# A searched order for a fused attention and gated-MLP kernel: every piece of work named, freely ordered, with PSUM banks and copy engines dealt by the same search

## The chip, the cores and the metric

The kernel runs on one core of a Trainium2 chip. The metric is the device time of one execution in microseconds (us). With one core there is no second die to compare with; an execution counts as slow when it lies over 1.5% above the fastest of its kernel. Every run of a changed kernel quoted here is in the fast state. The kernel before was not always: its executions spread from 307 to 314 us, and 11 of the 37 on record are slow. That is why each comparison below uses the fast runs of the kernel before from the same chip and the same rounds.

## The reference, cut to what matters

```python
def phi(x):                                   # q and k: 8 x 8 x 576 x 64
    proj = np.einsum('bhsd,df->bhsf', x, w_phi)
    proj = proj - np.max(np.abs(proj), axis=-1, keepdims=True)
    return np.concatenate([np.exp(proj), np.exp(-proj)], axis=-1)
q_p, k_p = phi(q), phi(k)
kv  = np.einsum('bhsf,bhsd->bhfd', k_p, v);   z = np.sum(k_p, axis=2)
num = np.einsum('bhsf,bhfd->bhsd', q_p, kv)
den = np.einsum('bhsf,bhf->bhs', q_p, z)[..., None] + 1e-06
x   = (num / den), heads side by side         # 8 x 576 x 512
h = gelu_tanh(x @ w_in);  u, v = halves of h
v_n = (v - mean) / sqrt(var + 1e-06) * g_ln   # layer norm over the features
v_s = np.einsum('ts,bsd->btd', w_sg, v_n) + b_sg
out = x + (u * v_s) @ w_out
```

## The kernel before

The kernel is cut into 1659 pieces, each with a kind (one letter) and a block (one digit, the batch). A long string names the order in which the program records them. Each engine then runs its own pieces in that order; between engines semaphores keep the data dependencies that the recorded order implies.

```python
def op(kind, b, f, *args):
    pieces.setdefault(kind + str(b), []).append((f, args))
...
for x in map("".join, zip(ORDER[::2], ORDER[1::2])):
    f, args = pieces[x].pop(0)                # pieces of one kind and block: first come, first served
    f(*args)
```

Three groups of pieces carry the argument. The first is the k and q projection of one slot and four heads ("n"), whose k result, one PSUM bank of 128x512, has three readers: a maximum on DVE ("r") and two exponentials on ACT ("e", one for each sign).

```python
def project(j, i, n0, n1, h0, h1):            # piece "n"
    kk, qq = ps1(), ps1()                     # two PSUM banks, taken from the string BANKS
    ...
def reduce(j, i, name, dst, n0, n1, h0, h1):  # piece "r": DVE
    src = T[name, b, j, i]
    ...
    nc.vector.tensor_reduce(out=dst[:, n0, h0:h1], in_=src.rearrange("p (h x) -> p h x", h=4),
                            axis=AX.X, op=ALU.max, apply_absolute_value=True)
def exps(j, i, e, n0, n1, h0, h1):            # piece "e": ACT
    ...
    src = T["kk", b, j, i]
    nc.scalar.activation(out=kp[:, e, 4 * i:4 * i + 4].rearrange("p h x -> p (h x)"), in_=src, func=AF.Exp,
                         scale=(1.0, -1.0)[e])
```

The second is the gathering of `w_sg`, 15 small copies on DVE with an inner step of 5 ("Q"), and beside it POOL's products of v with the exponential factors ("s").

```python
def pick(m):                                  # piece "Q": DVE, SBUF to SBUF
    ...
    nc.vector.tensor_copy(out=wp[0:nr, n0:n1].rearrange("p t (i j) -> p t i j", j=2),
                          in_=w9[:, :, :, m:m + 6:5])
def times(e, x0, n0, n1, h0, h1):             # piece "s": POOL, SBUF to SBUF, 128x1024
    ...
    nc.gpsimd.tensor_tensor(out=VX[e][:, h0:h1, x0:x0 + nn, 0:64], in0=T["vs", b][:, h0:h1, n0:n1, :],
                            in1=VX[e][:, h0:h1, x0:x0 + nn, 64:65].broadcast_to([128, hh, nn, 64]), op=ALU.mult)
```

The third is the copies whose engine is free: `move` and `engine` take the next letter of a string (v for DVE, a for ACT, p for POOL).

```python
def engine(usual):
    return {"v": nc.vector, "a": nc.scalar, "p": nc.gpsimd}[next(alts, usual)]
```

## Time and profile before

| | kernel before |
|---|---|
| median before the prediction, 3 runs | 308.34 us (307.46 to 310.44) |
| span of the profiled run | 305.4 us |
| busy, whole span: PE, DVE, ACT, POOL | 261.5, 253.1, 249.7, 161.3 us |
| busy share from 40 to 240 us: PE, DVE, ACT | 94%, 91%, 97% |
| ACT table loads | 28 |

The page's busy lines, the stretches and the chain are read in the prediction. Three more views also belong here and are shown here for the comparison later. First the gathering copies by form (line, engine, operation, shapes, count, then busy us, mean ns of one, idle us before them):

```profile
L316 DVE COPY wp<-wn 128x384 f16<-128x384 f16 x4 | 1.5, 380 | 0.0
L316 DVE COPY wp<-wn 64x128 f16<-64x128 f16 x4 | 1.2, 303 | 0.0
L316 DVE COPY wp<-wn 128x128 f16<-128x128 f16 x4 | 1.2, 297 | 0.0
```

Then the waits between the two readers of the k bank (who waited, on whom: us in all, times, longest):

```profile
DVE MX L388 <- ACT kp L407: 2.5, 3, 1.4
...
ACT kp L407 <- DVE MX L388: 0.2, 1, 0.2
```

DVE and ACT read the same 72 banks, and in the whole run they held each other up for 2.7 us. How that looks in time (start, us, what, idle before it in brackets):

```profile
22.68 4.65 ACT L407 ACTIVATE kp<-banks 128x512 f16<-128x512 f32 x9
...
23.87 6.06 DVE L388 TENSOR_REDUCE MX<-banks 128x4 f32<-128x512 f32 x10
```

Nine exponentials in a row on ACT lie beside ten maxima in a row on DVE, with no idle time on either: neither waits for the other.

### The profile page before, as it was taken

The numbers are of one execution on the slowest core, as the hardware profiler recorded it, in microseconds if no ns is written. First come the engines' busy times: TensorE is split into PE (matmuls) and PEld (weight loads), VectorE is DVE, ScalarE is ACT, GpSimd is POOL, SyncE is SP. The second block draws the span as 40 slices with busy tenths as digits, with TensorE's granted clock in tenths as the row PEclk, the third lists the DMA queues.
The fourth block names the chain that finished last, engine by engine and source line by source line (L and its number), as shares of the span: only waits on it lengthen the run. The fifth ranks groups of instructions, "written<-read, shape, count | busy, mean of one in ns | idle before, by whom it ended". The sixth has DMA issues, their size and how long they took to land.

```text
span 305.4 us, 8083 instructions
## 1 busy us (share of the span) xinstructions
PE 261.5 (86%) x3209; PEld 157.7 (52%) x3209; DVE 253.1 (83%) x606; ACT 249.7 (82%) x428; POOL 161.3 (53%) x155
## 2 busy tenths in 40 slices
PE   0146298897789999999998999999999999999993
...
DVE  3289849997899699999899899998998796877862
ACT  0049489999899899999999999999999989994210
POOL 8763999937058924803289567042694360044100
...
GB/s 160 221 205 197 59 42 222 173 192 144 255 55 0 123 228 265 105 150 278 190 79 12 45 236 5 256 126 71 13 26 141 115 29 71 2 78 29 38 108 165
DMA packets 60550, 37.48 MB, mean 123 GB/s; under 512 B 31648, under 2 KB 57184, under 8 KB 60512
## 3 DMA queue, kind: packets, MB, share of 16 engines
...
q0 software_dynamic: 22816, 11.81, 30.5%
q8 instruction: 25, 0.41, 0.6%
...
## 4 chain that ended last, share of the span: by engine, by line
PE 44%; ACT 23%; DVE 13%; POOL 8%; DMA 7%; issue 4%; ACTq 0%; DVEq 0%; SPq 0%; POOLq 0%
PE banks L681 9%; ACT kp L407 7%; PE banks L610 5%; POOL vx L424 5%; ACT qp L516 4%; PE banks L707 4%; DVE MX L388 4%; PE banks L530 4%; PE banks L479 4%; PE banks L506 4%; PE banks L660 4%; PE banks L382 3%; DMA qks<-in_k_dram 3%; ACT uT L673 2%; ACT vt L619 2%
## 5 line engine op out<-in xcount | busy, mean ns | idle before, releaser
L424 POOL TENSOR_TENSOR vx<-vs,vx 128x1024 f16<-128x1024 f32 (+1 forms) x48 | 77.9, 1645 | 53.5 <-ACT vx L414 45.4
L388 DVE TENSOR_REDUCE MX<-banks 128x4 f32<-128x512 f32 x144 | 91.8, 677 | 5.7 <-PE banks L382 2.6
L407 ACT ACTIVATE kp<-banks 128x512 f16<-128x512 f32 x144 | 77.7, 634 | 1.7 <-PE banks L382 1.4
L516 ACT ACTIVATE qp<-banks 128x1024 f16<-128x1024 f32 (+1 forms) x90 | 72.8, 904 | 1.9 <-PE banks L530 0.9
L681 PE MATMUL banks<-WsgT,vt 128*128 128x512 f16 (+1 forms) x256 | 38.6, 286 | 0.6 <-DVE uT L696 0.2
L382 PE MATMUL banks<-wk,qkT 64*128 64x128 f16 x288 | 30.5, 232 | 7.8 <-DVE qkT L143 5.2
L382 PEld LDWEIGHTS <-qkT 64*128 64x128 f16 x576 | 18.9, 100 | 26.5 <-issue 19.3
L610 PE MATMUL banks<-Win,xT 128*128 128x512 f16 x128 | 31.4, 379 | 0.7 <-DVE xT L143 0.3
L660 PE MATMUL banks<-xT,Win 128*128 128x512 f16 x128 | 32.0, 380 | 0.0
L530 PE MATMUL banks<-kvz,qp 128*128 128x65 f16 x640 | 29.7, 194 | 2.3 <-ACT qp L516 0.9
L550 DVE TENSOR_TENSOR xs<-banks,rd 128x256 f16<-128x256 f32 x80 | 31.1, 411 | 0.6
L530 PEld LDWEIGHTS <-qp 128*128 128x128 f16 x640 | 25.3, 98 | 11.3 <-issue 2.9
L382 PE MATMUL banks<-wq,qkT 64*128 64x128 f16 x288 | 29.7, 232 | 1.0 <-DVE MX L388 1.0
L479 PE MATMUL banks<-vx,kp 128*128 128x65 f16 x640 | 28.4, 195 | 1.2 <-POOL vx L424 0.9
L479 PEld LDWEIGHTS <-kp 128*128 128x128 f16 x640 | 24.7, 99 | 6.5 <-issue 1.2
L696 DVE TENSOR_TENSOR uT<-banks,uT 128x512 f16<-128x512 f32 x32 | 21.8, 685 | 6.2 <-PE banks L681 5.8
L208 PE MATMUL banks<-ident,qk 128*128 128x128 f16 x112 | 11.8, 277 | 16.8 <-DVE qk L143 16.5
L707 PE MATMUL banks<-Wout,uT 128*128 128x512 f16 x96 | 25.9, 379 | 0.0
L506 PE MATMUL banks<-qkT,wqm 66*128 66x512 f16 x72 | 22.8, 383 | 3.6 <-DMA qkT<-hl 2.1
L651 POOL TENSOR_TENSOR vt<-vt,g_bc 128x1024 f16<-128x1024 f16 x7 | 15.6, 2222 | 19.1 <-DVE vt L645 19.1
L681 PEld LDWEIGHTS <-vt 128*128 128x128 f16 x256 | 17.0, 98 | 14.7 <-issue 1.2
L407 ACT ACT_TABLE_LOAD x6 | 7.7, 1283 | 19.6 <-DVE qkT L143 19.5
...
## 6 DMA issues: line engine op xcount, KB each, us to landing
...
```

Of the source, the lines that this page charges most:

```text
L382: nc.tensor.matmul(dst, qkT[p:p + 64, n, h, :], w[p:p + 64, :], start=True, stop=True)
L388: nc.vector.tensor_reduce(out=dst[:, n0, h0:h1], in_=src.rearrange("p (h x) -> p h x", h=4), axis=AX.X, op=ALU.max, apply_absolute_value=True)
L407: nc.scalar.activation(out=kp[:, e, 4 * i:4 * i + 4].rearrange("p h x -> p (h x)"), in_=src, func=AF.Exp, scale=(1.0, -1.0)[e])
L424: nc.gpsimd.tensor_tensor(out=VX[e][:, h0:h1, x0:x0 + nn, 0:64], in0=T["vs", b][:, h0:h1, n0:n1, :], in1=VX[e][:, h0:h1, x0:x0 + nn, 64:65 ...
L479: nc.tensor.matmul(T["pkv", b, h // 3][:, c:c + 65], kp[:, e, x, :], VX[e][:, h, sh if n == SH else n, :], start=(n == 0), stop=(n == SH))
L506: nc.tensor.matmul(d, wqm[0:66, :], T["qkT", b][0:66, n, h:h + 4].rearrange("p h x -> p (h x)"), start=True, stop=True)
L516: nc.scalar.activation(out=dst, in_=T["pp", b, n, s], func=AF.Exp, scale=(1.0, -1.0)[e])
L530: nc.tensor.matmul(dst[h // 4][:, 65 * (h % 4):65 * (h % 4) + 65], qp[:, e, h, :], kvz[:, h, e, :], start=(e == 1), stop=(e == 0))
L610: nc.tensor.matmul(pv, T["xT", b][:, c, n * 128:n * 128 + 128], Win[:, c, DF2:DFF], start=(c == 0), stop=(c == 3))
L660: nc.tensor.matmul(pu, Win[:, c, d * 128:d * 128 + 128], T["xT", b][:, c, :], start=(c == 0), stop=(c == 3))
L681: nc.tensor.matmul(dst, lhs[:, d * 128:d * 128 + 128], WsgT[:, m, t0:t1], start=(m == 0), stop=(m == 4))
L707: nc.tensor.matmul(po, u[:, d, cs], Wout[:, d, :], start=False, stop=(d == 3))
```

## The change

Its intent is to find, by a long search, an order in which no engine waits. Each piece now has its own name (kind, block, number), so pieces of one kind and block can swap; the PSUM banks and the engines of the free copies come out of the same search. No piece is added or removed. The three strings are new from end to end.

```diff
+INDEX = "0123456789abcdefghijklmnopqrstuvwxyzABCDEFGHIJKLMNOPQRSTUVWXYZ"
 ALTS = (
-    "pvvpvvavvvvaavapvvvvaavvaaavvvvavvaaavvvavavvvvaaaavvvaavvvaavvvvvvvvpvaapppavvvvpavpvaavvavvvvaavvavppvapaa"
...
 ORDER = (      # 1659 names of two characters become 1659 names of three
...
 BANKS = (      # 500 digits, all dealt anew
...
     def op(kind, b, f, *args):
-        pieces.setdefault(kind + str(b), []).append((f, args))
+        n = count[kind + str(b)] = count.get(kind + str(b), -1) + 1
+        pieces[kind + str(b) + INDEX[n]] = (f, args)
...
-            if i == e == 0:                      # three such places: whichever piece comes first takes the tile
+            if ("kp", b, j) not in T:
...
-    for x in map("".join, zip(ORDER[::2], ORDER[1::2])):
-        f, args = pieces[x].pop(0)
+    for x in map("".join, zip(ORDER[::3], ORDER[1::3], ORDER[2::3])):
+        f, args = pieces.pop(x)
         f(*args)
```

More of the change, by code (lines that the diff above doesn't have):

```diff
@@ L30 @@
 VPOOL = ()
+INDEX = "0123456789abcdefghijklmnopqrstuvwxyzABCDEFGHIJKLMNOPQRSTUVWXYZ"
 ALTS = (
-    "pvvpvvavvvvaavapvvvvaavvaaavvvvavvaaavvvavavvvvaaaavvvaavvvaavvvvvvvvpvaapppavvvvpavpvaavvavvvvaavvavppvapaa"
-    "aavvavaavvavavavapvpvvvpa"
+    "aavvavvavapavavvvvvvavvvvvppavaavvvvvvvpvpppaaavvaavvvpvppavvvavvvaavapvppppavvvavvavvpvvvavpavvvavpvpvpvvvv"
+    "vvvpaappaavvavvvvvapvvvpa"
 )
 ORDER = (
-    "F0v0a0v0a0v0a0D0a0a0a0a0a0a0a0m0a0a0L0m0a1t0F0t0a1a1a1c0m0c0n0a2e0m0a2t0a2e0n0c0r0t0r0e0n0e0c0n0r0e0n0e0r0e0"
@@ L37 @@
-    "r0n0e0r0a2e0r0e0n0e0r0f0r0f0n0s0e0r0e0t0e0r0e0r0s0e0c0r0n0r0n0e0a2r0e0a2r0f0f0e0s0r0e0r0r0r0s0f0f0h0i0m1j0s0"
-    "m1A0j0t1s0t1s0c1t1s0c1n1A0c1t1s0e1e1p0s0c1n1r1k0k0r1m2v1x0p0k0r1x0v1k0x0k0l0p0x0r1p0n1x0k0r1x0p0A0k0x0l0A0x0"
-    "r1n1x0A0k0m2u0x0a3l0e1d0r1u0a3e1p0t2e1d0g0a3g0x0n1r1a3u0x0r1f1t2L0f1c2p0d0r1L0g0c2a4n1Q0u0Q0a4e1T0d0x0r1p0x0"
-    "g0s1x0r1u0u0x0X0p0e1d0d0t2g0x0g0n1c2s1x0p0e1r1y0u0x0y0r1x0d0Q0u0a4z0T0e1t2d0g0a4e1g0u0c2Q0a4T0u0d0Q0z0t2d0g0"
-    "g0a4T0e1m3V0e1m3a5e1y0X0e1t3V0X0X0z0n1G0c2V0r1V0r1a5G0B0V0G0B0G0U0B0G0T0B0f1n2a5n2B0r2f1s1X0r2e2r2n2e2U0r2e2"
@@ L42 @@
-    "r2s1U0e2r2e1h1e2b0b0b0i1e2a5e1b0k1b0N0k1N0H0U0j1j1k1k1U0v2l1k1H0v2C0k1n2H0C0C0v2l1C0H0C0p1t3E0H0k1x1n2E0k1E0"
-    "r2W0r2f2r2l1W0f2r2x1M0u1u1e2p1d1M0e2d1x1g1n2g1u1r2n2x1d1r2e2p1g1s2e2r2u1W0e2d1r2x1g1n2s2M0W0x1r2e2r2n2f2y1f2"
-    "M0u1s2e2u1d1e2z1O0d1e2g1g1e2r2p1s2P0y1r2x1n2z1u1u1x1d1r2V1d1g1e2u1g1u1f2r2f2V1e2s2d1d1e2m4O0e2s2g1G1g1y1m4a6"
-    "O0a6z1t4G1B1s2V1P0B1P0s2V1b1G1b1a6V1B1G1s2b1h2B1O0G1s2i2k2B1P0a6n3b1k2b1e3n3a6N1N1U1a6W0e3U1M0e3r3e3U1r3H1k2"
-    "C1U1C1C1C1U1l2C1k2E1H1j2H1E1n3H1k2j2E1H1r3W1v3e3r3v3k2M1k2t4l2p2r3n3r3x2W1r3x2r3W1M1e3e3n3M1k2e3n3r3l2p2f3W1"
@@ L47 @@
-    "r3f3s3e3r3x2n3r3x2M1u2S0s3r3e3O1S0e3d2r3S0e3n3g2S0e3m5p2e3O1r3a7x2r3a7O1m5f3f3x2s3P1u2u2e3d2h3u2g2e3i3p2P1s3"
-    "W1d2P1d2j3g2x2g2p2j3M1y2u2x2z2u2t5a7k3d2d2g2k3x2a7g2k3k3l3u2x2k3d2u2g2p3d2k3g2x3u2l3u2p3d2d2x3g2k3y2g2k3x3z2"
-    "n4u3l3y2x3d3r4u3V2d3g3e4g3e4u3z2V2t5G2d3r4u3V2g3d3g3V2G2B2G2V2B2G2S1B2p3S1G2B2y3u3v4x3n4z3u3d3B2v4O1d3g3v4g3"
-    "m6y3x3p3m6b2b2z3P1u3b2b2b2u3r4x3S1V3d3d3r4S1x3V3g3N2t6g3e4u3N2n4e4d3u3g3e4n4d3U2e4g3e4r4y3e4r4U2z3r4t6G3V3r4"
-    "C2V3C2C2G3V3E2B3G3B3U2G3B3G3n4H2C2U2C2H2E2B3H2n4B3O1H2r4f4U2r4E2n4r4f4W2r4s4P1e4r4S1e4n4r4S1e4W2M2s4e4r4e4U3"
@@ L52 @@
-    "e4M2f4f4r4W2e4s4b3e4b3b3b3b3W2H3M2N3s4n4M2n4H2r4O2r4e4N3n5r4U3r5f4r5f4e5s4P2n5e5s4e4r4n5e5h4s4U3e5i4e5s4r5e5"
-    "U3j4e4s4r5j4U3e4r5s4H3k4r5n5k4r5k4v5O2l4H3v5r5H3k4H3O2P2e5C3S2C3p4C3S2W2E3k4x4C3O2C3E3M2x4n5P2P2p4e5k4r5E3S2"
-    "n5x4k4l4S2k4r5x4W3r5f5f5r5n5s5l4u4e5M3W3e5d4r5e5u4e5g4p4s5M3e5n5d4x4r5W3g4x4r5W3M3f5f5r5s5e5u4y4e5M3p4z4u4d4"
-    "e5u4g4h5O3x4d4d4s5i5g4x4j5p4g4u4P3n6j5x4u4d4m7k5v6O3g4x4d4r6v6u4g4e6v6k5r6k5P3p5d4m7e6u4S3y4x5l5S3k5g4k5d4t7"
-    "x5z4k5p5l5u4k5g4x5u5d4n6g4k5d5r6x5O3g5l5r6n6e6u5P3r6p5e6y4d5r6e6u5u5g5e6V4t7d5d5z4x5n6g5V4g5x5r6n6r6f6u5f6O3"
@@ L57 @@
-    "s6e6r6e6d5r6e6V4g5e6P3s6n6G4V4S3r6S3r6U4G4p5B4G4y5B4V4G4B4H4u5z5U4B4G4d5b4b4g5x5B4y5b4W3b4b4z5u5N4u5M3U4N4x5"
-    "d5d5g5g5e6u5n6e6d5n6g5e6u5V5e6d5g5e6r6U4e6C4H4C4O3C4E4r6r6U4H4r6y5H4V5C4H4C4G5E4z5n6P3B5G5V5S3r6f6S3U5B5E4r6"
-    "n7f6n6b5s6e6b5r7W4e6r6e7W4r6e7s6f6M4f6e6U5r7e6M4n7G5V5s6r7r7h6s6V5i6G5U5s6H5B5j6G5B5U5s6j6H5B5H5n7s6b5b5W4H5"
-    "b5r7e7s6r7k6W4M4v7N5N5e7v7k6M4p6e7n7e7k6x6r7k6O4r7l6x6k6O4C5P4C5e7C5k6C5P4O4C5l6E5S4e7p6E5S4P4n7x6E5W4r7k6x6"
-    "M4n7r7k6O4l6r7f7f7r7s7e7n7P4p6r7e7W5S4r7x6S4s7n7M5x6W5r7e7r7W5f7f7M5s7e7e7u6M5p6e7h7W5d6e7i7s7e7g6j7u6M5u6u6"
@@ L62 @@
-    "j7u6d6d6x6U5d6g6d6O5g6g6x6g6k7P5k7H5u6p6d6O5g6u6x6P5k7k7d6y6l7S5p7k7g6S5O5z6x6y6P5k7z6k7l7u6u6d6u6x7g6k7x7d6"
-    "p7d6g6p7V6l7g6x7x7p7y6x7u7x7z6u7u7x7u7d7d7V6d7g7x7d7g7G6g7V6g7V6G6V6B6G6B6G6u7p7B6G6p7u7p7B6x7O5B6p7d7U6d7P5"
-    "x7g7S5W5g7x7b6b6S5u7b6x7b6b6y7M5U6x7N6d7N6g7x7u7x7u7d7y7x7g7U6z7d7z7H6u7g7O5d7g7y7H6C6C6V7H6C6z7E6P5V7S5G7V7"
-    "G7S5B7V7C6G7C6E6B7V7G7B7U6B7G7b7E6U7H6B7W6b7b7b7H7b7N7N7W6M6W6M6U7M6W6H7C7C7C7U7M6E7U7H7C7O6C7H7E7O6E7P6O6P6"
-    "W7S6P6S6W7M7W7M7W7M7O6M7U7P6O7H7S6O7S6P7W7P7U6M7S7W6H6S7O7M6O7P7O7P7S7P7S7S7S7"
+    "a03a00a01a02a04a05m00m01t01a0aa09a07a0bD00F00F01m03t00c00a08c01n02a06a10a25r05a13n00r01n03n01a11e05m02t03e01"
@@ new lines @@
+    "r06r00e06e03r04e07t04c04e04e02t02r02a12a24c03n09a22r0iv00e00r07f00e0in08A01r0hf01e0ga23n06e0jc02m11r0gr0de0h"
+    "f05a20n07f04m10a21r0fA02e0cn05r0jt11v01c11t10r0bn04s01r0ce0br03s04e08r09s00c10e0ft12r08e09t13r0an12r0ev02s05"
+    "h00m21f02r15e0ei00s07n11s08f03c13n10r13j00e13m20e10k00A03k01k02c12A00e0ar12e0de14e12j01e15p00r11k03t20p04p01"
+    "A04r14e11s03r10l00p05t23s02c20c23k05n13a30k04k06x02x00x01a33x0ak07Q00p03a42x0bx08l01a31T00p06Q04l02u05x03p02"
+    "Q02r17x06t22x07u01x09u04d05x04X00e17r16f11x05L01g05c22L00u00d00x0da32T02d01d04x0cg04u03s09n16e16d03e1cp08X02"
@@ new lines @@
+    "g01g03u02r1dx0gs06L02v11n15g00t21p07t24c21e1dr1be1au06x0hp09a45x0ed02Q01r1cx0fu08d06g02v10m30g06y00m31u07t30"
+    "d07c24x0ia44x0jr1aT04g07X04e1by01u09n14d09z01d08g09n17e1eg08V01r18z00f10e1fe18r1ef13n22r25y02z02Q03r24r1fV04"
+    "f12V00s12r19s11U01e19G01V02H01G00n23G02h10B01r27V03i10b01T01G04G03B04B00n20e20j11s10B03b04e21X01n21r23t31e25"
+    "B02s13b00a40r22U00b02b03e23e24e26r21U02U03k15k13r20k14r26N00k11N01l11k12k10k16e27e22C00C02C04C01T03U04X03H02"
+    "H00k17j10l10l12E00p10u11u10d11d10C03a43g10p11v22H03H04n27g11x11E02a41y10r2fz10x10n26r2du13d13g13u12e2ed12g12"
@@ new lines @@
+    "E01W00x13M00x12p12W01n24r2eu14f21e2fm40x14v20m41a64r2cx15r29M01r28d14W02M02g14u15p13W03e2de2cd15M03n28O01g15"
+    "r2gx17x16v21u19n29t41e28y11r2ha53e29O00r2ie2jP01d19r2jf20e2ig19f24u16z11P00e2hs21a50u18f25u17d18V14n25d16d17"
+    "g16e2ag18g17n30e2br31y12z12e2ge30s20S01V10s24O02r2af23f22r2bV13r30h20i20s25e31P02n32r34V11V12r35G10B10G11B11"
+    "G14U12s26G12j20a51b10U10G13s22s27U13s23B14H10H12H13s28U11U14j21n33s29H11b14n31H14B13b13B12b12b11e32N10r36N11"
+    "k26k20k22O03r37v31r33k21e36C12e35e34C14W04t40k27e33k25k24l20a71P03n37k23C13C10C11M04e37l22r32E10p20n35e3eE11"
@@ new lines @@
+    "x20E12S00x21l21e3fr3er3fr3bv30W13f31W12e3aM13p21n34r39x22x23M12W10e3bp22W11M10n36r3au22r38a52e39e38M11r3cu20"
+    "O11x25x24a65S02S03d22m50u23r3df32m51h30P11d23g22p23d20u21s31O10a61i30f30d21g21g23u25g20p24x27d25W14x26s30e3c"
+    "e3dP10j30u24u26g25d26d24f33g26g24x28j31M14u27d27O12x29y21s32z21p30y20u29z20g27u28d28P12t51n40x30s33V20d29g29"
+    "k31x31e40k30r40a62p31e41a63k37g28y22r41k32k34V24x33k35l30x32k36z22V23G24G20l32V22B24B20t50b20k33G23b24V21G22"
+    "l31u32B22u35B23u31G21u33S11d35p32x35d31g35u30g31d32x34d33u34g32g33d34O13p33d30g30n43x36b23g34y30b22a60u36u37"
@@ new lines @@
+    "r47v40x37P13z30U22y31d37d36B21z31g37b21g36u39d39m60N20N21g39u38d38n42e46U21n45r45S10e45e4aV30g38C21V31r44e44"
+    "C20V34r46e47y32r4aS12e4br4bz32U34H22U20C22H34G30C23n41C24G31U30E20r43n47G34H21H20v41B30r4fH30U31U23H31U24H23"
+    "H24r4er42E21f40f41n49E22v42m61B31b30s40e4er4je4fn46b31r4dW20s41S13M20W24n44e4je4ir48W21M24r4cf43e42e43M21V32"
+    "r4ie4dr49V33n48e4gW22r4hr4gO14e48e4he4cf42s43n50B34M22r50f45e49r51f44P14W23h40i40U32s47M23n52G33S14G32U33H32"
+    "O23n51s44r54j41r55H33s46b34e50B33B32O20s48b33S15e54n53P23b32j40e52s45s42O22r53t61r56r57O21e55e51k47P22k46k41"
@@ new lines @@
+    "e57k42r52s49e56v50P21v51e53k40l40p40x41k45k44l42N30x40k43n54e59f51N31C31C30p41C32t60C34C33l41r59n56P20E31E30"
+    "e5dr5df50e58S23E32x43x42n57r5fW31e5cr58W32M31p42S21S22r5er5cx44x45s50n55e5er5br5aW30u43W34M32M34M30f52h50e5b"
+    "s51i50e5aW33d43s52u42g43M33f53p43d42u40u45s53e5fj51a70O32d45p44d40g45x46u44P32d44x47g40x48x49g42g44u46u47d47"
+    "g47k56k57l52d46k53j50p50k55g46k54p51u49l51u48d48g48x50x51k50x53k52d49g49k51l50n60r60y41r61u41z41u53d53O31e60"
+    "x52d41e61u52m70S20p52P31n62g41d52a73g52y42V41g53r65z42u55d55y40r64u54V42x54v62z40d54x55e65e64G42n61V40g55G41"
@@ new lines @@
+    "V43G43g54r62r63B42U40B41G40H40V44B43u56u57p53B40O33d56G44d57b43B44g57n63y51x57b42a72v61b40b41x56v60g56P33S32"
+    "e67b44e66e63O30P30z51r67u50d50e62V51n67r66f61g50r6fu58u59U42n65m71e6eN40e6bN41C40d59U44d58g58g59y52e6ae6fC41"
+    "U43r6aV50S33z52r6eu51H44G51H42r6bC42U50C44d51V52E40C43E42n66G50g51r6dE41H43G52U53n69S31H50n68r6cH53r6ir6gf65"
+    "s61s67O34P34r6hW40f60t70W42n64e6cf64M40r6je6dr68M42s60S30V53e69e68f63y50W43r69h60t71e6ie6jf62z50B52s63e6gs68"
+    "n71e73i60V54j61W41r72U41B51e6hb51s64s65U52e72H41G54j60H52U51M43r73n74B50M41H51B54r79G53s62B53O42s69k62b52S34"
@@ new lines @@
+    "p60x61S35k64b54b50b53x60P42N50p61x63r78k60N51k61l60C52C51k66x62k63C50k67k65C54O41p62l61l62e78P41e79u60u62d60"
+    "u63g60d62x64O43d63x65p64x69g63n76g62C53r7dW44x68u61E50r7cP43u64d64M44O40g64d61g61u65d65P40u68e7de7cS43g65u69"
+    "d68p63E52E51x67d69g68x66n73e76W52n72r76s66g69e77M52W50e75S42r75r77y60z60n70M50y61r71z61u66d66W53g66n77e74u67"
+    "W51v71r74r70V64d67e70f71r7fM53e71n75V60S41g67e7fV61e7br7ey62r7ae7ee7af70U54r7bz62f72h70i70M51f73G60G64v70s71"
+    "S40W54V63G61B61s70V62s72b61j71B60O51s73O50H54M54G63j70p70p73P51G62B62B64B63b62b64b63b60N60p71p72k76x70x73k70"
@@ new lines @@
+    "x77x75k71x74k73k77l72k75k74x76k72l70U62x72l71P50u71d71u74g71u70p77x71d70d74u75u73g70u72p76x7dO53g74p74d72d75"
+    "g75x7fx7cx7eO54P53x79d73O52p75x78N61C60g72g73y70y71P52z70u76z71S50x7bU61S51C62u78C63S52d76E61C61V71x7au77H61"
+    "U74E60d78d77P54S55H74V70g76u79d79g77V74U60g79G74G70H62C64g78E62y72W61z72G71B71b71B74B70b70V72b74G72B72V73G73"
+    "b72B73b73N70N71W62M62S54H60U63M61U72U71W60H63S53C71C74E72H71C73W63M60C72U73U70M63H72O63C70E70O61O60E71O62W70"
+    "P60W73P62W71P63H73P61S60S61M73W72H70M70M71W74M72O72S63O73P72S62P73W64O71P71S72U64H64M74M64S73O70P70S71S70O74"
@@ L67 @@
+    "P74S75S74"
 )
 BANKS = (
-    "010213450126573401265370400120312456017236051720562407546073056703567135673267124032513214562741562053604275"
-    "647056347063276301576412670145706210210213045676135271031657342561045136420671453104370346124031267036457230"
-    "243562460124056137015136213406524735610313456102427013632507164215172450672301534012054701204751602564067452"
-    "346702356472350170431462371623123645020367106213745603564072401324613405021450675042715475246017456740645236"
-    "24016205132467014201345267201420351601701201232301201201010210210230"
+    "010213452637470231534754025645020243216703547241564321054230641720526703426531420761765423651237657021405412"
@@ L74 @@
+    "701401560562372057432501634501234654127632465645102643217420651274641620371240720374267430176324016710706134"
+    "276032745270561470156370237135403576456041543234076203671526375346543056732632015034602374301762470601237614"
+    "023127634507650126571061723562043523741065203464376127345170372540625406523624501456704352675016341573265074"
+    "61541076451203237015360475413074031645715035354323523401701076016041"
 )
@@ L115 @@
     ctx.enter_context(tc.manual_schedule())
-    pieces = {}
+    pieces, count = {}, {}
     bank = map(int, BANKS)
     def op(kind, b, f, *args):
-        pieces.setdefault(kind + str(b), []).append((f, args))
+        n = count[kind + str(b)] = count.get(kind + str(b), -1) + 1
+        pieces[kind + str(b) + INDEX[n]] = (f, args)
     def ps():
@@ L472, in sums @@
         def sums(h):
-            if h % 3 == 0:
+            if ("pkv", b, h // 3) not in T:
                 T["pkv", b, h // 3] = ps1()
```

4 lines of the change are left out of this document (2 added, 2 removed).

## The prediction

> **What bounds the kernel now.** I read first the busy shares and the forty slices of the page, then the same busy times over chosen stretches, then the chain of waits and the groups by form.
>
> ```profile
> PE 261.5 (86%) x3209; PEld 157.7 (52%) x3209; DVE 253.1 (83%) x606; ACT 249.7 (82%) x428; POOL 161.3 (53%) x155
> ...
> PE   0146298897789999999998999999999999999993
> ...
> DVE  3289849997899699999899899998998796877862
> ACT  0049489999899899999999999999999989994210
> POOL 8763999937058924803289567042694360044100
> ```
>
> Three engines stand within 12 us of each other, so no single one explains 305.4 us. The slices show three stages: a start in which only POOL and the DMA queues work, a long middle, and an end in which ACT runs dry and PE is full. The stretches put numbers on it (columns: span, then busy us and instruction count of PE, PEld, DVE, ACT, POOL, then PE clock, DMA share, GB/s):
>
> ```profile
> 24.00:44.00 20.00, 11.81 (x127) 8.46 (x124) 15.50 (x27) 13.86 (x29) 16.10 (x16) 1.00 0.82 102
> ...
> 40.00:240.00 200.00, 187.67 (x2438) 113.46 (x2436) 181.23 (x435) 194.90 (x333) 115.63 (x106) 1.00 0.72 133
> ...
> 280.00:300.00 20.00, 20.00 (x160) 10.25 (x157) 14.66 (x25) 2.56 (x5) 2.23 (x2) 1.00 0.20 79
> ```
>
> In the 200 us from 40 to 240 ACT is busy 97%, DVE 91%, PE 94%. PE's figure is flattering: in a dense stretch a 512-column matmul takes 216 ns from start to start, a 65-column one 31 ns, a pair of 64-row projections 56 ns, and 664 x 0.216 + 1280 x 0.031 + 288 x 0.056 plus about 30 us of small ones is near 231 us, not 261.5. So PE has slack in the middle, ACT has almost none. In the chain that ended last the start goes over DVE, then POOL (start, us, what):
>
> ```profile
> 4.73 8.33 DMA qks<-in_k_dram
> ...
> 15.12 2.61 DVE WsgT L306 x4
> ...
> 18.74 1.29 DVE qkT L143 x2
> ...
> 27.65 3.83 POOL vx L424 x2
> 31.47 1.37 POOL qks L167 x2
> 32.85 3.83 POOL vx L424 x2
> ...
> 47.28 4.94 DMA wn<-in_moe_w_sg_dram
> ```
>
> The first k lands at 13.1 us, DVE then works about 5 us on the bias rows of WsgT before it copies the first qkT, and from 27.6 to 47 us POOL is the last link.
>
> **What the Trainium skill says.** "ScalarE: Activation LUTs", section "What ACT_TABLE_LOAD costs", gives 1283 ns for a load and 2.66 us with the drain for each switch of table set. The trace agrees on 1283 ns; it shows no drain: the ACT operation before a load at 104.76 ends at 104.75, the next starts at 106.06. Since ACT operations in a row overlap by about 0.1 us, I take 1.4 us a switch. "SBUF — State Buffer", section "Who interferes with whom", says that POOL and a DVE copy in a two-port mode lock each other out of one port pair. The before trace cannot separate that from plain duration, so I count it as a risk only. "Perfetto Trace Analysis", section "Optimization Strategy", says that interleaving regimes with different most-contended engines may improve performance; that is what a new order tries, and the stage numbers above (ACT 97% in the middle, 13% near the end) say there is something to interleave.
>
> **The change part by part.** The multiset of pieces is the same: 1659 in both orders, PE has the same 6412 rows. What differs is order, banks, which engine makes a free copy, and how often ACT switches its table.
>
> (1) Table loads. Listing ACT's instructions gives 28 loads before and 22 after. 6 x 1.4 = 8.4 us less ACT time, all after the first 40 us.
>
> ```profile
> L619 ACT ACT_TABLE_LOAD x7 | 9.0, 1283 | 0.1
> ...
> L141 ACT ACTIVATE osb<-banks 128x512 f32<-128x512 f32 x17 | 10.3, 628 | 4.0 <-PE banks L707 4.0
> ...
> L141 ACT ACTIVATE qkT<-banks 128x1024 f16<-128x1024 f16 x7 | 7.0, 1051 | 3.8 <-PE banks L208 3.8
> ...
> L141 ACT ACTIVATE kvz<-banks 128x260 f16<-128x260 f32 x6 | 2.4, 407 | 0.1
> L143 POOL COPY qk<-qks 128x1280 f16<-128x1280 f16 x2 | 2.5, 1264 | 1.0 <-DMA qks<-in_q_dram 1.0
> ```
>
> (2) Copies that leave ACT: 6 kvz x 0.407 = 2.4, 3 osb x 0.628 = 1.9, 2 WsgT about 1.4, 2 of x 4x64 x 0.47 = 0.9, net 3 of qkT x 1.05 = 3.2. Together 9.8 us.
>
> (3) Copies that ACT gains: four merges of q and k (two of 1280 columns, one of 2048, one of 2560). ACT takes 0.634 us for 512 columns and 1.062 for 1024, so 0.836 ns a column: 1.27 x 2 + 1.91 + 2.34 = 6.8 us. They all stand near the head of ACT's order, where ACT waits anyway (19.5 us before its first exp, 6.1 us of 24 to 44).
> ACT in sum: -8.4 - 9.8 + 6.8 = -11.4 us; without the merges and the qkT copies of the first blocks, about -15 us in the middle.
>
> (4) DVE. It loses 8 merges of 2048 x 0.679 = 5.4, 3 of 2560 x 0.940 = 2.8, two or three gains 1.5; it gains 6 kvz x 0.42, 3 osb x 0.68, 3 net qkT x 0.68, 2 WsgT x 0.43, 2 x 0.41: 8.3. In sum about -1.5 us: 251.5.
>
> (5) POOL. It gets 7 merges of 2048 (1.89 us each, between 1.264 for 1280 and 2.312 for 2560) = 13.2, two more of 2560 = 4.6, two vm and one vt gains x 1.2 and 2.2 = 4.7, and drops two of 1280 = 2.5: +20 us, so 181 of 305. It waits 45.4 us for the vx factors today, so it has room, but not in the start.
>
> (6) The start. Six loads of the first heads are the first six in both orders, so the first k should land near 13 us again. Before, POOL's merges stand between its DMA issues; after, all twelve loads of block 0 are issued first (about 0.72 us each). The bias block on DVE stands ahead of the first qkT copy in both orders, but its load is now first on SP's queue, ahead of v, so it should run while DVE waits for k. I expect the first exp 1 to 1.5 us earlier, about 18 us. Between the first and the last k-sum, POOL's factor products for the next slots stand later and the issues are spread; I put 1.5 to 2 us on the ramp.
>
> (7) The end. After the last qp exp in the order stands PE work of about 30 us before and 28 us after, by the same per-matmul times. The closing store is unchanged. I put 0 to 1 us on it.
>
> On the path: ACT has 195 of 200 us in the middle and loses 15. If ACT alone set the pace the middle would shrink by about 15. But DVE has 181 there and loses almost nothing: to fit 185 us it would have to run at 98%, as full as ACT does today. I take two thirds, 9.5 us. Sum: 1 + 1.5 + 9.5 + 0.5 = 12.5 us. 308.3 - 12.5 = 295.8, say **296 us**, 4% less.
>
> **The rivals.** First: DVE takes over as the bound. It is busy 91% in the middle, and each wait there (0.9 us at most in nearly all rows) is a bank that PE fills. Then most of ACT's 15 us turns into ACT idle time, the gain is 3 to 5 us, and the result is 303 to 305. For it: DVE's load hardly changes. Against: the order is new everywhere, and freed ACT time lets banks come free sooner for DVE too.
> Second: POOL becomes the wait. A merge of 2048 on POOL takes 1.9 us where DVE took 0.68, it feeds the transposing DMA (8.6 us to landing), and it stands in one queue with the factor products that PE's k-sums need and with all q and k loads. A late merge could cost several us in each block: 300 to 310. For it: POOL is full from 40 to 60 us. Against: later it is busy only 30 to 75% of a stretch, and loads lie blocks ahead.
> Third: the search found more than the load counts show. The floor from DVE is about 17 us before its first reduce, 244 us of work, 5 us of store, 266; an order that brings DVE to 96% over the whole middle gives 285 to 290. For it: 22 us of DVE idle time and 25 us of PE idle time lie after 14 us. Against: the kernel before was already well packed.
>
> **Range and chances.** A 2% gain means under 302.2. The main sum lands 6 us below that. DVE as the bound, or POOL's waits, spoil it perhaps one time in five; the third rival reaches 285 to 290 about as often. Range 288 to 304. Faster 0.78, same 0.20, slower 0.02: total work falls and no engine's load rises except that of the idlest.
>
> **What would show it.** Step 1: 22 loads of 1283 ns. Steps 2, 3: ACT busy near 238, and in the middle below 95%. Step 4: DVE busy near 251 and its share in the middle up from 91% to 94 to 96%. Step 5: POOL near 181, with qk merges of 1.9 to 2.3 us and waits for vx factors shortened. Step 6: first exp near 18 us. Step 7: the last 20 us again full on PE. I am wrong if PE or ACT show new waits on POOL's merges or vx of over 5 us, if DVE copies on both sides of POOL's grow longer, or if ACT's idle time in the middle grows by as much as its work falls.

## The result, and the profile after

| | before | after |
|---|---|---|
| median of the fast runs | 308.34 us (3 runs, 307.46 to 310.44; a fourth, 314.41, is slow) | 318.59 us (4 runs, 317.19 to 319.78) |
| ratio, with 95% interval | | 1.0317 (1.0233 to 1.0401), slower |
| span of the profiled run | 305.4 us | 317.1 us |
| ACT table loads | 28 | 22 |

A ratio here and below is the mean time of one kernel's fast runs over the mean time of the other's in the same rounds, so it is not quite the ratio of the medians quoted beside it.

The page of the kernel after, its busy line and slices:

```profile
PE 270.1 (85%) x3209; PEld 163.2 (51%) x3209; DVE 261.6 (82%) x608; ACT 242.8 (77%) x410; POOL 178.6 (56%) x165
...
PE   0067887776789999899999989999999979999993
...
DVE  3368979989969799877889999988989867988772
ACT  0369877892878999798999999998979969885201
POOL 8368994285576883880478848332687706402300
PEclk9996557897979999999999999999999999999999
```

ACT and POOL moved the way foretold: ACT fell by 7 us, POOL rose by 17. Yet DVE rose by 8.5 us with nearly the same work (608 instructions in place of 606), and PE by 8.6. The stretches of the same kernel (columns: stretch, length, busy us and count of PE, PEld, DVE, ACT, POOL, then clock, DMA share, GB/s):

```profile
24.00:44.00 20.00, 15.07 (x165) 10.89 (x163) 17.98 (x30) 17.18 (x31) 18.21 (x19) 0.55 0.77 108
40.00:240.00 200.00, 182.70 (x2216) 109.21 (x2213) 176.77 (x408) 173.03 (x296) 126.09 (x106) 0.95 0.68 128
70.00:74.00 4.00, 0.00 (x0) 0.01 (x1) 4.00 (x5) 1.21 (x3) 4.00 (x3) 0.99 0.32 71
```

The first line says that the start got better: in the same 20 us PE began 165 matmuls, against 127 before, and ACT worked 17.2 us, against 13.9. The second says that the middle got worse in a particular way. ACT did 296 instructions where the kernel before did 333, and no engine is full: PE 91%, DVE 88%, ACT 87%. So nothing has become the bound in the sense of a full engine; the engines wait for one another. The third line is a hole, in which PE does nothing at all while DVE and POOL are both "busy" without a break. The same hole as instructions in order of time, cut to those that tell it:

```profile
66.96 7.73 POOL L442 TENSOR_TENSOR vx<-vs,vx 128x1024 f16<-128x1024 f32 x4 [1.20 <-issue]
...
67.33 5.54 DVE L334 COPY wp<-wn 128x384 f16<-128x384 f16 x3
...
72.80 1.87 DVE L406 TENSOR_REDUCE MX<-banks 128x4 f32<-128x512 f32 x3
74.12 0.26 PE L400 MATMUL banks<-wk,qkT 64*128 64x128 f16 x1 [4.13 <-DVE MX L406]
...
74.99 1.91 PE L628 MATMUL banks<-Win,xT 128*128 128x512 f16 x4
...
76.94 0.60 ACT L637 ACTIVATE vt<-banks 128x512 f16<-128x512 f32 x1 [5.74 <-PE banks L628]
```

POOL's four products take 1.93 us each. Next to them DVE's three small copies, one of each form, take 5.54 us, 1.85 each, nearly the length of a product, where the kernel before needed 0.3 to 0.4 us for one. The maxima behind them come late, PE waits 4.13 us for a bank, and ACT 5.74 us for PE. After the hole PE runs slower for a while ("cold" below): four matmuls of `Win` take 1.91 us, against 1.03 for four of the same form at 68.97. By form, in the kernel after:

```profile
L334 DVE COPY wp<-wn 128x384 f16<-128x384 f16 x4 | 5.0, 1256 | 0.0
L334 DVE COPY wp<-wn 128x128 f16<-128x128 f16 x4 | 2.8, 710 | 0.0
L334 DVE COPY wp<-wn 64x128 f16<-64x128 f16 x4 | 2.8, 692 | 0.0
```

All 15 copies together took 12.9 us, against 5.1 before: a growth of 7.8 us, while DVE as a whole gained 8.5. The waits of the kernel after, in the form shown of before:

```profile
ACT kp L425 <- DVE MX L406: 15.7, 19, 1.9
DVE MX L406 <- ACT kp L425: 10.8, 15, 2.7
ACT vt L637 <- PE banks L628: 7.1, 2, 5.7
PE banks L400 <- DVE MX L406: 5.9, 5, 4.1
```

The first two lines have grown: 26.5 us in which one reader of a k bank waits for the other, against 2.7. In time:

```profile
22.21 2.56 ACT L425 ACTIVATE kp<-banks 128x512 f16<-128x512 f32 x5 [1.29 <-DVE MX L406]
24.80 2.48 DVE L406 TENSOR_REDUCE MX<-banks 128x4 f32<-128x512 f32 x4 [0.83 <-ACT kp L425]
```

ACT waits until DVE has read a bank, then DVE until ACT has. Neither result is of use to the other; they only share the bank. The Trainium skill, page "PSUM — Partial Sum Buffer", section "PSUM bank collisions raise a hardware error", says that two engines must not access one bank within the same partitions at the same time, two readers included, and that the program has to guard each bank by semaphores. The trace agrees in so far as the program waits here for nothing but the other reader; no run shows what an unguarded pair would do. Which of the two goes first is what the recorded order says. For the 72 k banks I read it off the two order strings: in the kernel before, the maximum is recorded ahead of both exponentials 52 times, behind both 19 times and between them once; in the kernel after 32, 17 and 23 times.

So there were two suspects, the copies beside POOL (A) and the readers of the k banks (B), and three lesser ones: the merges on POOL, which my prediction had named as a rival, PE's cold start (the clock row above reads 5 to 7 in slices 4 to 7), and the exponential-maximum-exponential pattern as such. The cold start was a weak suspect: the row of the kernel before reads 9 in those slices, yet its pairs of 64-row projections too came every 105 to 107 ns for the most part until about 44 us, and every 56 ns after that.

### The profile page after: what moved, and what is told of

It is laid out like the page before. It is cut to its first block, busy times and chain, and to the rows that moved or that the text cites. A ratio compares the mean times of both kernels' runs of the same rounds, so it can differ in the third digit from the quotient of the medians.

```text
span 317.1 us, 8012 instructions
## 1 busy us (share of the span) xinstructions
PE 270.1 (85%) x3209; PEld 163.2 (51%) x3209; DVE 261.6 (82%) x608; ACT 242.8 (77%) x410; POOL 178.6 (56%) x165
## 4 chain that ended last, share of the span: by engine, by line
PE 52%; DVE 19%; ACT 14%; DMA 8%; issue 4%; POOL 2%; ACTq 0%; POOLq 0%; DVEq 0%
PE banks L699 9%; DVE MX L406 8%; PE banks L678 7%; ACT kp L425 7%; PE banks L725 5%; PE banks L628 5%; PE banks L548 5%; DMA qks<-in_q_dram 5%; PE banks L524 4%; PE banks L497 4%; PE banks L400 3%; DVE wp L334 3%; ACT qp L534 3%; PE banks L720 2%; PE banks L631 2%
## 5 line engine op out<-in xcount | busy, mean ns | idle before, releaser
L406 DVE TENSOR_REDUCE MX<-banks 128x4 f32<-128x512 f32 x144 | 93.6, 681 | 13.3 <-ACT kp L425 10.8
L425 ACT ACTIVATE kp<-banks 128x512 f16<-128x512 f32 x144 | 80.4, 618 | 17.8 <-DVE MX L406 15.7
L534 ACT ACTIVATE qp<-banks 128x1024 f16<-128x1024 f32 (+1 forms) x90 | 71.6, 880 | 6.0 <-PE banks L524 5.5
L161 POOL COPY qk<-qks 128x2048 f16<-128x2048 f16 (+1 forms) x11 | 22.4, 2045 | 36.2 <-DMA qks<-in_k_dram 9.7
L699 PE MATMUL banks<-WsgT,vt 128*128 128x512 f16 (+1 forms) x256 | 39.7, 290 | 3.5 <-DVE xs L568 2.2
L548 PEld LDWEIGHTS <-qp 128*128 128x128 f16 x640 | 26.7, 101 | 13.5 <-issue 5.8
L628 PE MATMUL banks<-Win,xT 128*128 128x512 f16 x128 | 32.5, 387 | 0.4 <-ACT kp L425 0.4
L226 PE MATMUL banks<-ident,qk 128*128 128x128 f16 x112 | 12.1, 286 | 18.8 <-ACT qk L159 17.2
L497 PE MATMUL banks<-vx,kp 128*128 128x65 f16 x640 | 25.6, 198 | 1.1 <-ACT kp L425 1.1
L669 POOL TENSOR_TENSOR vt<-vt,g_bc 128x1024 f16<-128x1024 f16 x8 | 17.3, 2161 | 14.4 <-DVE vt L663 14.4
L637 ACT ACTIVATE vt<-banks 128x512 f16<-128x512 f32 x32 | 17.9, 597 | 7.4 <-PE banks L628 7.1
```

The costliest lines, as they stand in the source:

```text
L497: nc.tensor.matmul(T["pkv", b, h // 3][:, c:c + 65], kp[:, e, x, :], VX[e][:, h, sh if n == SH else n, :], start=(n == 0), stop=(n == SH))
L534: nc.scalar.activation(out=dst, in_=T["pp", b, n, s], func=AF.Exp, scale=(1.0, -1.0)[e])
L548: nc.tensor.matmul(dst[h // 4][:, 65 * (h % 4):65 * (h % 4) + 65], qp[:, e, h, :], kvz[:, h, e, :], start=(e == 1), stop=(e == 0))
L628: nc.tensor.matmul(pv, T["xT", b][:, c, n * 128:n * 128 + 128], Win[:, c, DF2:DFF], start=(c == 0), stop=(c == 3))
L699: nc.tensor.matmul(dst, lhs[:, d * 128:d * 128 + 128], WsgT[:, m, t0:t1], start=(m == 0), stop=(m == 4))
```

## The experiments

Fourteen kernels ran; all their runs were in the fast state and all passed the comparison with the reference. A table first, then each with its edit. "Before" is the median of the fast runs of the kernel before in the same rounds; the ratios are those of the record.

| run | edit | median us | before | ratio (95%) |
|---|---|---|---|---|
| e1_ree | after, 23 patterns undone | 317.85 | 308.48 | 1.0281 (1.0211 to 1.0352) |
| e2_ere | before, 22 patterns put in | 322.22 | 308.48 | 1.0433 (1.0358 to 1.0508) |
| e3_merge | after, merges from POOL to DVE | 321.73 | 308.48 | 1.0411 (1.0338 to 1.0483) |
| e4_wp | after, gathering as a maximum | 311.18 | 308.48 | 1.0057 (0.9973 to 1.0142) |
| f1_wp_ree | e4 and e1 | 311.01 | 307.20 | 1.0101 (1.0058 to 1.0144) |
| f2_before_wp | before, gathering as a maximum | 310.41 | 307.20 | 1.0086 (1.0023 to 1.0148) |
| f3_before_wp_ere | f2 and e2 | 317.93 | 307.20 | 1.0333 (1.0265 to 1.0401) |
| f4_wp_warm | e4, PE kept warm at the start | 311.5 | 307.20 | 1.0137 (1.0076 to 1.0198) |
| g1_wp_still | e4, k maxima read no bank | 300.19 | 307.76 | 0.9749 (0.9692 to 0.9807) |
| g2_before_wp_still | f2, k maxima read no bank | 309.09 | 307.76 | 1.0038 (0.9977 to 1.0099) |
| g3_wp_hoist | e4, maxima moved forward | 335.08 | 307.76 | 1.0871 (1.0817 to 1.0925) |
| g4_wp_merge | e4 and e3 | 318.61 | 307.76 | 1.0334 (1.0265 to 1.0403) |
| h1_still | after, k maxima read no bank | 307.09 | 307.88 | 0.9941 (0.9854 to 1.0028) |
| h2_sorted | e4, recorded as g1 had run | 306.85 | 307.88 | 0.9928 (0.987 to 0.9986) |

**e1_ree: the pattern undone in the kernel after.** Each of the 23 triples recorded as exponential, maximum, exponential becomes maximum, exponential, exponential; the names swap places in the order string, for instance of projections 2 and 0 of block 0:

```diff
-n01 a11 e05 m02 t03 e01 r06 r00 e06 e03 r04 e07
+n01 a11 r04 m02 t03 r00 r06 e01 e06 e03 e05 e07
```

> The changed kernel with one thing undone: in 23 projections the k bank is read by ACT, then DVE, then ACT again (exp, max, exp); here the DVE max is swapped ahead of both exps, so each engine has the bank once. Engines, banks and everything else stay. Theory 1 (the swaps made ACT and DVE wait for each other at one bank: 15.7 us of ACT waits on the max, 10.8 us of DVE waits on the exp): these waits fall below 8 us in sum and the time falls from 318.6 to 311 to 314. Theory 2 (POOL's merges and the loads behind them) and theory 3 (DVE copies locked out by POOL, one stall of 5 us near 67 us): the waits fall but the time stays within 2 us of 318.

Measured 317.85 us: less than 1 us better. The waits did not vanish, they moved to one side:

```profile
ACT kp L425 <- DVE MX L406: 16.1, 14, 3.7
DVE MX L406 <- ACT kp L425: 7.9, 8, 2.4
```

So undoing the pattern does not pay. It is not a clean test of who reads first, though: the swap also moves maxima forward in DVE's own order and exponentials back in ACT's, and a late maximum now holds up both exponentials.

**e2_ere: the pattern put into the kernel before.** In 22 triples of the kernel before, the maximum and the first exponential swap places in the order string (the edit of e1 read backwards).

> The kernel before with the opposite: 22 of its projections get the order exp, max, exp on the k bank (23 with the one it has), 7 of them in block 0, the same blocks as in the changed kernel where that is safe. Theory 1: ACT waits on the max and DVE waits on the exp rise from 2.7 us to over 12 us in sum and the time rises from 309 to 313 to 317. Theories 2 and 3: within 2 us of 309.

Measured 322.22 us, 4% slower. This run proved less than it seems, because it set off the other suspect too:

```profile
56.23 4.29 DVE L334 COPY wp<-wn 64x128 f16<-64x128 f16 x1
56.60 1.95 POOL L442 TENSOR_TENSOR vx<-vs,vx 128x1024 f16<-128x1024 f32 x1
```

One gathering copy took 4.29 us. A second product followed on POOL without a break and ended at 60.43, and the copy ended at 60.52. So such a wait can be longer than one POOL instruction. (The 1.26 us "each in the mean" in the text recorded for f3 is this one copy, averaged with the three others of its form.) Shifting things by a few microseconds was enough to bring a copy beside POOL's work. An experiment on the order needs the copies out of the way first; f3 below does that.

**e3_merge: the merges taken off POOL.**

```diff
 ALTS: 11 of its letters, the merges of q and k that POOL makes
-    "aavvavvavapavavvvvvvavvvvvppavaavv..."
+    "aavvavvavavavavvvvvvavvvvvvvavaavv..."
```

> The changed kernel with all 11 POOL merges of q and k made by DVE (the order is not touched). DVE gets 7 x 0.68 + 4 x 0.94 = 8.5 us more, POOL 22 us less. Theory 2 (POOL's late merges hold up the loads and the qkT of the next blocks): 311 to 314 in spite of DVE's load. Theories 1 and 3: 318 to 324, as DVE has 8 us more and nothing waits less.

Measured 321.73 us, 3 us more than the kernel after. POOL's merges are not the cause; to have them there pays.

**e4_wp: the gathering in a form that doesn't need the shared port.** The Trainium skill, page "SBUF — State Buffer", section "Who interferes with whom", says that a copy on DVE can take a port pair that it shares with POOL, that one of the two then waits for the whole of the other's instruction, and that `tensor_reduce` on this chip never does. A maximum over an axis of length 1 is a copy in the guise of a reduction.

```diff
-nc.vector.tensor_copy(out=wp[0:nr, n0:n1].rearrange("p t (i j) -> p t i j", j=2),
-                      in_=w9[:, :, :, m:m + 6:5])
+nc.vector.tensor_reduce(out=wp[0:nr, n0:n1].rearrange("p t (i j) -> p (t i) j", j=2),
+                        in_=w9[:, :, :, m:m + 6:5].rearrange("p t i j -> p (t i) j").unsqueeze(3),
+                        axis=AX.X, op=ALU.max)
... (the same in the branch for the fifth piece)
```

> The changed kernel with the 15 gathering copies of the w_sg pieces on DVE written as a max over an axis of length one: the same values, same engine, same place, but an operation that should not need the port shared with POOL. Theory 3 (three of them took 5.5 us at 67 us while POOL made four products of 1.9 us; the group of 15 took some 12 us against 4.5 in the kernel before): the 15 take under 7 us, none over 0.8 us, the 5.5 us stall of PE and ACT near 70 us goes, and the time falls by 4 to 6 us to 313 to 315. Theories 1 and 2: the copies shorten but the time falls by under 2 us.

Measured 311.18 us, 7.4 less than the kernel after, more than the 4 to 6 expected. By form:

```profile
L334 DVE TENSOR_REDUCE wp<-wn 128x384 f16<-128x384 f16 x4 | 2.2, 540 | 0.0
L334 DVE TENSOR_REDUCE wp<-wn 128x128 f16<-128x128 f16 x4 | 1.1, 278 | 0.0
L334 DVE TENSOR_REDUCE wp<-wn 64x128 f16<-64x128 f16 x4 | 1.1, 267 | 0.0
```

The 15 took 5.5 us in place of 12.9, a difference of 7.4 us of DVE time, and the end came 7.4 us sooner. Three of them lay beside a merge on POOL, which is as long as in the kernel after:

```profile
63.38 1.89 POOL L161 COPY qk<-qks 128x2048 f16<-128x2048 f16 x1 [6.14 <-DMA qks<-in_k_dram]
...
63.55 0.92 DVE L334 TENSOR_REDUCE wp<-wn 128x384 f16<-128x384 f16 x3
```

In the kernel after three copies beside such a merge, at 57.72, took 1.90 us. The trace agrees with the page: the copy of 384 columns took 1.63 us beside the merge, the reductions didn't wait. What stayed are the waits between the readers:

```profile
ACT kp L427 <- DVE MX L408: 12.9, 18, 1.7
DVE MX L408 <- ACT kp L427: 10.9, 15, 2.7
```

**f1_wp_ree: e4 with the edit of e1.** The edits are the two above together.

> The changed kernel with the w_sg copies as max (311.2 us in its run) and also no projection in the order exp, max, exp (23 swapped to max, exp, exp). Theory 1 as a second cause, hidden behind the lock stall in the first pair of runs: ACT waits on the max and DVE waits on the exp fall from 24 us to under 15 in sum and the time falls by 3 to 8 us to 303 to 308. Rival (the waits move elsewhere, as when it was undone alone and gave 0.7 us): 310 to 312.

Measured 311.01 us, the same as e4 (311.18); the 3 to 8 us that I had expected did not come. This confirms e1 with the copies out of the way: the waits were 15.7 and 7.7 us, 23.4 in place of 23.8.

**f2_before_wp: the control for e4.** The edit of e4 in the kernel before, where the copies were not held up.

> Control: the kernel before with the w_sg copies as max. Its 15 copies took 5.1 us and would take about 5.5. If the 7.4 us in the changed kernel came from the lock and not from the new operation being better in itself, this is within 1.5 us of 308.5.

Measured 310.41 us, 0.9% slower than the kernel before, just outside the 1.5 us expected (one merge on DVE took 2.30 us in this run, where the longest of its form took 1.30 before). So the reduction is not a faster gathering by itself (a row of 384 takes 540 ns, the free copy 380); what it saved in e4 was the lock. And with the copies cured in both, the two orders are level: 311.18 us new, 310.41 old.

**f3_before_wp_ere: f2 with the edit of e2.**

> The kernel before with the w_sg copies as max and 22 projections in the order exp, max, exp. Alone that order cost 13.7 us, but three of its w_sg copies then took 1.26 us each in the mean, so part of it was the lock. If the order itself costs time: 314 to 318. If the lock made most of it: 309 to 312.

Measured 317.93 us, 7.5 more than f2, now without held-up copies. The waits between the readers rose from 2.7 us in the kernel before to:

```profile
DVE MX L408 <- ACT kp L427: 4.6, 8, 1.1
ACT kp L427 <- DVE MX L408: 4.6, 7, 1.9
```

The swap of 22 maxima with exponentials costs the old order 7.5 us. How much of that is the shared bank is not shown, since the swap changes DVE's and ACT's own orders too. Moving a maximum behind an exponential in one finished order does harm; e1 and f1 say that moving it back in another does not heal. That each order is built around the places of its pieces would explain both, but no run tests it.

**f4_wp_warm: PE's cold start.** 235 transposes that no one reads, before the first real one:

```diff
+            for _ in range(235 if b == 0 and not T.get("warm") else 0):
+                nc.tensor.transpose(pt[:, 0:128], ident[:], ident[:])
+            T["warm"] = True
```

> The changed kernel with the w_sg copies as max and 235 idle transposes of the identity on PE before its first real one, which end before the first q and k arrive. It asks what the slow PE clock of the first 45 us costs (pairs of projections 105 ns apart in place of 56). If PE's clock sets the pace of the start: projections 56 ns apart from 17 us on, and 2 to 5 us off 311. If DVE and ACT set it: spacing halves, the time stays within 1.5 us.

Measured 311.5 us, no gain over e4. The pairs of 64-row projections did come every 56 ns until 20 us, as in the warm middle, but from 24 us on they were spaced much as in e4, mostly 105 to 107 ns. So PE's clock does not set the pace of the first microseconds of its work; the stretch from 24 to about 46 us was not made warm, and stays untested.

**g1_wp_still: e4 with the second reader taken away.** The 72 maxima of k read a constant tile in SBUF in place of the bank; the maxima of q stay. The arithmetic is wrong on purpose (it passes the comparison all the same).

```diff
+    still = consts.tile([128, 512], F32)
+    nc.vector.memset(still[:], 0.5)
-            src = T[name, b, j, i]
+            src = T[name, b, j, i] if name == "qq" else still
```

> The changed kernel with the w_sg copies as max, and the 72 maxima over the k bank read a constant SBUF tile of the same shape in place of the bank: a wrong result on purpose, the same number of DVE instructions of nearly the same length, but only ACT reads the k bank now. It asks what the hand-over of a bank between the two readers costs. Theory 1 (the program makes one reader wait for the other; ACT and DVE lose 24 us to it in the parent and the search placed the two close together, 3 places apart in the median where the kernel before has 9): both waits go and the time falls from 311 by 6 to 12 us. Rival (the waits are slack that another wait fills at once): within 3 us.

Measured 300.19 us, 11.0 less than e4 and 2.5% faster than the kernel before (the interval, 1.9 to 3.1%, does not quite clear the 2% of a verdict). DVE's work did not get shorter by it: the page has 256.1 us, against 254.5 in e4, and a maximum from the constant tile takes 673 ns, from a bank 679. Both waits between the readers are gone, and the middle fills (columns as in the stretches above):

```profile
40.00:240.00 200.00, 189.43 (x2446) 114.31 (x2446) 184.41 (x448) 185.66 (x314) 134.99 (x112) 0.97 0.67 130
```

PE did 2446 matmuls in these 200 us, the kernel after 2216, the one before 2438.

**g2_before_wp_still: the control for g1.** The same edit in f2.

> The same in the kernel before (wrong on purpose too), whose parent with the w_sg copies as max took 310.4 us and loses under 3 us to these waits. Theory 1: it falls by 1 to 3 us only, so less than the changed kernel does. Rival: both fall by about the same.

Measured 309.09 us, 1.3 less than f2, which the spread of the two (307.91 to 311.44, 309.44 to 311.58) does not tell from nothing. So what g1 took away, the second reader and all that hangs on it, was worth about 1 us to the old order and 11.0 to the new one.

The text recorded for g1 says that the search placed the readers closer together. My count was misread: the median of first exponential less maximum is 9 places in the kernel before and minus 3 in the kernel after. So the maximum moved from ahead of the exponential to behind it; the distance regardless of sign is 12 places before and 11 after.

**g3_wp_hoist: the maxima moved forward.** In the order of e4, 57 of the 72 maxima of k are moved forward, to at most six places behind their projection; 59 of the 72 then stand ahead of both exponentials.

```diff
-r05 a13 n00 r01 n03 n01 a11 e05 m02 t03 e01 r06 r00
+r05 a13 r04 n00 r01 n03 n01 a11 e05 r00 m02 r06 t03
```

> The changed kernel with the w_sg copies as max and each max over a k bank that stood over 6 places after its projection moved up to 6 places after it (57 of 72), so that DVE is through with the bank before ACT wants it, as in the kernel before. Correct result. Theory 1: ACT waits on the max fall from 13 to under 7 us and the time falls to 304 to 308. Rival (DVE, which runs in order, then waits for PE in their place): 309 to 314.

Measured 335.08 us, the slowest of all. DVE's pieces stay in the order in which they are recorded, so a maximum placed early makes everything behind it wait for PE (12.3 us, against 1.9 in e4):

```profile
ACT kp L427 <- DVE MX L408: 19.8, 23, 2.2
DVE MX L408 <- PE banks L402: 12.3, 18, 2.0
DVE MX L408 <- ACT kp L427: 10.7, 8, 2.8
```

Not all of the loss is that: a centring operation of the layer norm on DVE took 4.51 us in this run, where 0.40 is usual.

**g4_wp_merge: e4 with the edit of e3.**

> The changed kernel with the w_sg copies as max and the 11 merges of POOL made by DVE. With the copies stalled this cost 3 us. If the merges on POOL are a good part of the change: 313 to 317. If they hold up loads and transposes (theory 2): 306 to 309.

Measured 318.61 us, 7.4 more than e4. That is what having 11 merges on POOL is worth once the copies are out of its way. The waits between the readers rose by it too, from 23.8 to 30.6 us, and one merge on DVE took 1.75 us in place of 0.68.

**h1_still: the kernel after with the edit of g1 alone.**

> The changed kernel with only the 72 maxima over the k bank reading a constant tile (wrong on purpose), its w_sg copies left as they were. If the lock stall and the bank hand-over are two causes that add up: 318.6 - 11 = 306 to 309.5. If the lock stall hides the hand-over or the other way round: over 312 or under 304.

Measured 307.09 us, 11.5 less than the kernel after, with the gathering copies still held up:

```profile
L337 DVE COPY wp<-wn 128x384 f16<-128x384 f16 x4 | 3.7, 934 | 0.0
```

The kernels after, e4, h1 and g1 make a square. Curing the copies is worth 7.4 us with the second reader and 6.9 without; taking the reader away is worth 11.0 us with the copies cured and 11.5 without. The two causes add. The runs are from different chips, and 5 of the 11 runs of the kernel before were slow in this batch (306.97 to 313.16 in all), so the square holds to 2 us or so: by the ratios the copies are worth 2.6% and 1.9%, the readers 3.1% and 3.8%.

**h2_sorted: a right kernel with the readers in a better order.** The pieces of e4 are recorded in the order in which g1 had run them on the chip. Each engine keeps its own order, and each piece its bank (the string of banks is rewritten to that end). What changes is only which engine's access to a bank is recorded first: the order of maximum and exponential flips in 20 of the 72 k banks.

```diff
 ORDER = (      # the same 1659 names, sorted by their start in the trace of g1
-a03 a00 a01 a02 a04 a05 m00 ...
+a03 D00 a00 v00 a01 v01 a02 ...
```

> The changed kernel with the w_sg copies as max and with its pieces recorded in the order in which the run without the hand-over executed them, each on its own bank: no engine's own order changes, only which of the two readers of a k bank the program puts first. Correct result. If the hand-over costs time because the recorded order disagrees with the order in which DVE and ACT get there: ACT and DVE lose under 12 us to it (24 in the parent) and the time falls from 311 to 303 to 307, below the kernel before. If any order of two readers that close costs the same: 309 to 312.

Measured 306.85 us, ratio 0.9928: a right kernel, faster than e4 and level with the kernel before. The 0.7% of the ratio is within the 2% that count as the same, and I can reproduce it only with a run of 311.62 us of the kernel before that the record lists as slow; against the six fast runs (mean 308.20) it is 0.5%. The waits fell from 23.8 to 18.5 us:

```profile
DVE MX L408 <- ACT kp L427: 9.6, 16, 1.5
ACT kp L427 <- DVE MX L408: 8.9, 14, 1.5
```

No engine's order, bank or copy engine changed (I compared the two strings piece by piece), so the 4.3 us between e4 and h2 (1.3% by the ratios, on two chips) come from who reads a bank first. That supports the reading of g1, which took away more than the hand-over: its maxima need not wait for PE either (in e4 the waits of all maxima, of k and of q, on PE were only 1.9 us), and a bank comes free sooner. So 11 us is the most that the hand-over can have cost, and about 4 of it are shown to hang on the order of the two readers alone; the rest is not told apart. Distance is not what helped: the nearer exponential stands 7 places from its maximum in e4 and 6 in h2 (medians).

## Why the prediction was wrong

Predicted 296 us, range 288 to 304; measured 318.59. By its own steps:

- **Steps 1 to 3, ACT's work: right in kind, 5 us off in size.** There are 22 table loads of 1283 ns. ACT's busy time was to be near 238 and was 242.8; below 95% in the middle it was (87%).
- **Step 4, DVE: wrong.** 251.5 us predicted, 261.6 measured. The term that failed is the one left out with "so I count it as a risk only". The gathering copies grew from 5.1 to 12.9 us. I named longer DVE copies beside POOL's among the signs of being wrong, but priced no such copy. "The before trace cannot separate that from plain duration" was a misreading. The trace has one of eight like copies of the bias rows at 1.99 us, where four of the others took 0.22, and it ends 0.09 us after a merge on POOL:

```profile
15.74 1.99 DVE L306 COPY WsgT<-bhl 1x128 f16<-1x128 f16 x1
16.36 1.28 POOL L143 COPY qk<-qks 128x1280 f16<-128x1280 f16 x1
```

  Another 3 us came from the centring operation of the layer norm on DVE, which e4 doesn't change:

```profile
L663 DVE TENSOR_SCALAR vt<-vt,agg,y 128x512 f16<-128x512 f16 x32 | 14.4, 474 | 0.5 <-POOL y L659 0.5
```

  In the kernel before the same 32 took 11.4 us. The trace of the kernel after shows the larger part: two of the 32 took 1.26 and 1.76 us in place of 0.40, each beside a product on POOL and ending 0.15 us after it. One of them:

```profile
296.37 2.12 POOL L669 TENSOR_TENSOR vt<-vt,g_bc 128x1024 f16<-128x1024 f16 x1 [2.61 <-DVE vt L663]
...
296.88 1.76 DVE L663 TENSOR_SCALAR vt<-vt,agg,y 128x512 f16<-128x512 f16 x1
```

  That is 2.2 us of the 3, with the look of the copies' stall; no experiment took POOL's product away.
- **Step 5, POOL: right.** 181 predicted, 178.6 measured, and merges of 1.9 to 2.3 us. That the merges would be a wait, the second rival, was refuted by e3 and g4: without them on POOL the kernel is slower.
- **Step 6, the start: right.** The first exponential came at 19.80 us, against 20.81: 1.0 us earlier, where I had said 1 to 1.5. My "about 18 us" counted from the table load at 19.52 and not from the exponential behind it.
- **The sum over the path: wrong, and the larger error.** "I take two thirds, 9.5 us" weighed only how full DVE and ACT are. It had no term for the engines waiting for each other at a shared bank. DVE's share in the middle was to rise to 94 to 96% and fell to 88%. That term was at most 11.0 to 11.5 us (e4 to g1, after to h1), against about 1 in the old order; 4.3 us of it came back in h2 by recording the other reader first in 20 banks.
- **The first rival, DVE as the bound, wasn't it either.** It expected ACT idle time because DVE is full; ACT's idle time came, but DVE had 23 us of its own in the same 200.

With both causes taken away, the new order gives 300.2 us (g1, wrong on purpose), inside the predicted range and 4 us above the prediction: 318.6 less 7.4 for the copies less 11.0 for the readers. The old order with the same two edits takes 309.1 (g2). So some 9 of the 12.5 us that I reckoned with seem to be there, as far as g1, which took away more than the hand-over, can say. They were eaten by two costs that my sums did not hold: one lengthens DVE's copies, the other is a wait and shows in no engine's load.

Three things stay open: why the search recorded the readers in this order (it may not have priced the hand-over; nothing here shows what it priced), whether a right order exists that loses nothing to the hand-over, and how the 11 us of g1 divide between the hand-over and what else its edit freed. One small slip of the prediction bears on nothing: PE's rows are 6418 on both pages, not 6412.

## What to carry to other kernels

Busy shares tell which engine can be the bound, not what an order costs: list, for each buffer with two readers on different engines, which is recorded first and which engine will get there first, before you trust a sum of loads. Where small DVE copies lie near POOL work in SBUF, price each at the length of a POOL instruction (or of two in a row, as in e2), look in the trace for copies that already take far longer than others of their form, or write it in a form that is not held up, and control for that form's own cost. Test one suspect with the others out of the way: the runs that moved the order without curing the copies (e2) measured both.

## What the Trainium skill lacked or had wrong

- "SBUF — State Buffer", section "Who interferes with whom": right about who is held up. It does not say that POOL can pass a waiting copy twice: in e2 a copy that started 0.37 us ahead of a product on POOL, while POOL was issuing a load, ended only after that product and the next, 4.29 us in all.
- "PSUM — Partial Sum Buffer": it gives the rule that two readers of a bank must be kept apart, not its price. Here 72 banks with a reader on DVE and one on ACT cost about 1 us in one order and up to 11 us in another, with the same work.
- "ScalarE: Activation LUTs": the 1283 ns of a table load are right; the drain that it adds is not in the traces, where all but a few loads start 0.02 us after the operation before them ends, and the next operation 0.01 us after the load.
